# Attention and two MLPs on one core: the second MLP's low pieces on VectorE, casts left to GpSimd, decode slots and splits moved, a 32-byte pad

## The chip, the cores and the metric

The kernel runs on one core of a Trainium2 chip. The metric is the time of one execution in device microseconds. Five engines work side by side: PE (matrix multiply, with its weight loads shown as PEld), DVE (VectorE), ACT (ScalarE), POOL (GpSimd) and SP, which here only issues DMAs. Each engine takes its instructions in the order in which the program put them into its queue.

## The reference

Three stages follow each other: a random-feature attention, an MLP with a leaky rectifier, and a second MLP that multiplies two projections with each other.

```
q_p, k_p = (phi(q_s), phi(k_s))                      # batch 4, heads 8, 576 tokens, 64 wide
x = num / den                                        # -> 2304 tokens x 512
h = x @ w_in;  g = max(h, 0) + alpha * min(h, 0)     # 512 -> 2048
x = g @ w_out                                        # 2048 -> 512
a = x @ w_a;  b = x @ w_b                            # 512 -> 1536, twice
out = (a * b) @ w_out2                               # 1536 -> 512
```

Inputs and outputs are 32-bit; the weights arrive as 64-bit numbers, `raw` in the kernel.

## The kernel before, in words

**Pieces.** Every matrix operand is held as a high piece (a cast to the matmul's 32-bit format) and a low piece (what the cast left over). Each product of two operands is three matmuls: high with high, high with low, low with high. A weight piece therefore fills one slot of 2 x 512 numbers per partition, high half and low half.

**Decode.** `Decoder` turns the 64-bit weights into such slots while the matmuls run. Per weight tile POOL scales one half (`z`, line 196), DVE shifts, masks and multiplies (lines 212, 217, 219, 221), and DVE adds the two parts. For the second MLP the pieces go in groups of two (`quad`) that DVE also combines into sums and differences; then `stage` (line 235) makes the high and the low piece: a POOL cast (line 243), and two slots later a POOL subtract (`pool_tt`, printed with its helper's line 159). There are 20 such stagings in each of three phases of weights, 60 in all. The result goes straight into an open slot, or through the buffer `t` to DRAM and back (`store`, `fetch`). The decoder is a generator: each call of `D_.more(1)`, `D_.go` or `D_.fill` runs it to its next `yield`, which is one decode slot; where those calls stand in the code sets where the decode's instructions stand in each queue.

**First MLP.** Class `Mlp`; each step takes one block f of 128 hidden columns and a chunk of tokens. `first` (line 440) does the 12 matmuls of `h`, ACT and DVE form the rectifier, ACT makes `gh` (line 468), DVE makes `gl` (line 465), and `a_back` (line 498) does the 12 matmuls of each of two steps earlier. The first instance `A` (256 tokens) runs beside the attention until 256 us. The second, `X`, runs from 256 to 553 us in chunks of 512 tokens, but for one of 256 near the middle of its second half. At the last step of a chunk, the matmuls of a step follow only one step behind. `X` runs two decode calls around each rectifier (`D_.fill`) and three between its matmuls.

**Second MLP.** From 553 us on there are nine passes, n = 0 to 8: three weight phases (`ps`), each over three groups of 768 tokens (`tp`). A pass has two `dual`s (j = 0 and 1) and one `back`. A `dual` computes both projections of 256 hidden columns for 768 tokens as 2 x 2 blocks with seven products instead of eight (A11, S1, S2, S4, S3, A12, A22, p = 0 to 6): 7 x 2 x 6 = 84 matmuls of 384 columns (line 1067). What comes out in banks W, E and B is copied by ACT (`s1`, `e5`, `u2`, `u3`, `w7`) and added and multiplied by DVE. The four products `u2`, `s1`, `e5`, `w7` are then split into `gh` (ACT) and `gl` (DVE) by `split`; two of these splits are put into the list `later` and taken out by `drain`, at A11 and S1 of the next dual or at the first tile of `back`. `back` takes six tiles of 128 tokens, 12 matmuls of 512 columns each (line 1138), in which the first three tiles need `gl` of `u2` and `s1` and the last three that of `e5` and `w7`. It adds the earlier phases' part (`opl`, from DRAM) and stores.

**Combine.** Where the next pass takes other tokens (after n = 0, 1, 3, 4, 6, 7), the generator `combine` forms the seven left-hand operands of the next pass: sums on DVE, high pieces on ACT, low pieces for the two row halves k = 0 on DVE and k = 1 on POOL. One step runs after each product of the dual j = 1 from p = 3 on, the others one per tile of `back`.

**Where tiles lie.** Pools without a side fill the memory from the bottom, pools with `side=RIGHT` from the top. In the built program, every tile of the left side starts at a multiple of 64 bytes (slots 0 to 16, 4096 bytes each, the decoder's buffers, the operands of A11, S1 and S2). On the right side, all of `X`'s tiles, slots 17 to 26, `gh` and `gl` of the second MLP and the operands of S4, S3, A12 and A22 start 32 bytes past a multiple of 64; the attention's tiles there are mixed, most of them at multiples of 64. `X` takes its 32 slots in turn: blocks 0 to 7 from slots 0 to 15, blocks 8 to 15 from slots 16 to 24 and then 0 to 6.

Of the kernel before, what the change touches and what calls it, by code (L numbers as in the profile page):

```python
# [18 lines left out]
P = 128  # L19
# [40 lines left out]
def tile_kernel(ctx: ExitStack, tc: tile.TileContext, qT, kT, v1, omT, wbits, alpha, out):  # L60
    nc = tc.nc
    ctx.enter_context(tc.manual_schedule())
    scale = 1.0 / math.sqrt(math.sqrt(D))

    const = ctx.enter_context(tc.tile_pool(name="const", bufs=1))
    w1 = ctx.enter_context(tc.tile_pool(name="w1", bufs=1))
    dec = ctx.enter_context(tc.tile_pool(name="dec", bufs=2))
# [97 lines left out]
    class Decoder:  # L165
# [68 lines left out]
        def stage(self, q, src, cut=None):  # L234

            if cut != 1 and self.open(q):
                self.direct.add(q)
            t = slots[place(q)][2] if q in self.direct else dec.tile([P, 2, 512], F32R, tag="t", name=f"t{q}_{cut}", bufs=3)
            if cut is not None:
                o = 256 * cut if q in self.direct else 0  # L240
                t = t[:, :, o:o + 256]
            self.flush()
            nc.gpsimd.tensor_copy(out=t[:, 0], in_=src)
            load["pool"] += 1.5
            yield
            yield
            pool_tt(t[:, 1], src, t[:, 0].bitcast(F32), ALU.subtract)
            self.due = (q, cut, t)
            yield

# [144 lines left out]
    class Mlp:  # L395
# [48 lines left out]
        def a_front(self, ph, o, n, f, last, mid):  # L444
# [26 lines left out]
            if self.beside:  # L471
                self.beside(high, low)
            else:
                D_.fill()
                high()
                low()
                D_.fill()

        def a_back(self, ph, o, n, f, last_chunk):
            halves = self.pair and o < 2 * CI  # L480
# [463 lines left out]
    def combine(ps, tp):  # L944
# [8 lines left out]
        for i in range(len(A_NAMES) + 2):  # L953
            if i >= 2:
                nm = A_NAMES[i - 2]
                for k in range(2):
                    l = t_(xpools[nm not in EARLY], f"xl{nm}{k}", f"xl{ps}{tp}{nm}{k}", dt=F32R)
                    (pool_tt if k else vec)(l, src[k][nm], high[nm, k].bitcast(F32), ALU.subtract)
                    xs[nm, k] = (high[nm, k], l)
            if 1 <= i <= len(A_NAMES):  # L960
                nm = A_NAMES[i - 1]
# [77 lines left out]
    def split(ps, tp, j, i, c, g):  # L1039

        gh = t_(gp, f"gh{j}{i}{c}", f"gh{ps}{tp}{j}{i}{c}", dt=F32R)
        gl = t_(gp, f"gl{j}{i}{c}", f"gl{ps}{tp}{j}{i}{c}", dt=F32R)
        act(gh, g)
        vec(gl, g, gh.bitcast(F32), ALU.subtract)
        gs[j, i, c] = (gh, gl)

    def dual(ps, tp, j, last, gen=None, g0=0):
        nm_ = f"{ps}{tp}{j}"
# [6 lines left out]
        for p, nm in enumerate(A_NAMES):  # L1055
# [32 lines left out]
            elif nm == "S3":  # L1088
                for m in range(2):
                    act(keep(m, "u3", 1), W[m])  # L1090
                split(ps, tp, j, 0, 1, sb[0]["u2"])
            elif nm == "A12":
                for m in range(2):
                    vec(sb[m]["s1"], banks[m]["B"][:, :TN], sb[m]["s1"], ALU.add)
                vec(sb[0]["s1"], sb[0]["s1"], sb[1]["s1"], ALU.mult)
                for m in range(2):
                    vec(sb[m]["e5"], sb[m]["u3"], sb[m]["e5"], ALU.add)
            else:
                act(keep(0, "w7", 1), W[0])
                split(ps, tp, j, 0, 0, sb[0]["s1"])  # L1100
                vec(sb[0]["w7"], sb[0]["w7"], W[1], ALU.mult)
                vec(sb[0]["e5"], sb[0]["e5"], sb[1]["e5"], ALU.mult)
                later.append(lambda: split(ps, tp, j, 1, 1, sb[0]["e5"]))
                later.append(lambda: split(ps, tp, j, 1, 0, sb[0]["w7"]))
            if nm in ("A11", "S1"):
                drain()
            if gen and p >= g0:
                next(gen, None)
            D_.fetch()
            if last:  # L1110
# [13 lines left out]
    def back(ps, tp, last, gen):  # L1124
        for t in range(2 * TN // P):
# [6 lines left out]
            for j in range(2):  # L1132
                for f in (1, 0):
# [3 lines left out]
                    for w_, r_ in ((gh, wh), (gh, wl), (gl, wh)):  # L1137
                        nc.tensor.matmul(ob, lhsT=w_[:, cs], rhs=r_, start=(n == 0), stop=(n == 11))  # L1138
                        n += 1
                if j == 0 and f == 0:  # L1140
                    D_.more(1)
            passed(12 * 0.227)
            D_.fetch()
            if last and t == 2 * TN // P - 1:
# [17 lines left out]
    for n, (ps, tp) in enumerate(seq):  # L1162
# [3 lines left out]
        for j in range(2):  # L1166
# [7 lines left out]
                    load_o(tp, 0)  # L1174
                    load_o(tp, 1)
            else:
                dual(ps, tp, j, last, gen, 3)
        back(ps, tp, last, gen)
        if gen:
            for _ in gen:  # L1180
# [58 lines left out]
```

## Time and profile before

| what | us |
|---|---|
| median of three runs (992.7 to 994.15) | 992.73 |
| the profiled execution | 989.9 |
| its span, first to last instruction | 988.1 |
| PE busy in the span | 954.2 |
| DVE busy | 698.9 |
| POOL busy | 381.9 |

The profile comes from one execution, 0.3% faster than the median; the span leaves out 1.8 us around the program. Times in the trace count from the span's start. A busy PE is not PE at its peak, since the matmuls overlap and their pace is read from one start to the next.

### The profile page before, as it was taken

The page shows a single profiled execution, that of the slowest core. Times are in us where ns is not written, and L with a number is a line of the kernel's source. Part 1 is how long each engine was busy: PE and PEld are TensorE (multiplying, and loading weights), DVE is VectorE, ACT ScalarE, POOL GpSimd, SP SyncE. Part 2 cuts the span into 40 slices and gives each one's busy share as a digit, 9 for nine tenths or more (in the row PEclk, how much of TensorE's full clock was granted, in tenths as well). Part 3 has the DMA queues.
Part 4 walks back from the last instruction along what each step waited for, and adds up shares of the span by engine and source line. Part 5 has one row for each costly group of instructions (what it writes and reads, how often), then busy time and mean ns, then how long its engine had stood idle before and what let it go on. Part 6 is the DMA issues. An engine that isn't in the chain of part 4 may idle for free.

```text
span 988.1 us, 16903 instructions
## 1 busy us (share of the span) xinstructions
PE 954.2 (97%) x6486; PEld 848.7 (86%) x6486; DVE 698.9 (71%) x1276; ACT 445.0 (45%) x1094; POOL 381.9 (39%) x312
## 2 busy tenths in 40 slices
PE   8899999999999999998999989999999999999998
PEld 7788889999888888888888879899989898979796
DVE  5888855554547768688667988799588995573733
ACT  5877766654444443333333344443343431333340
POOL 3676700000066655437325646264155272030300
PEclk8999999999999999999999999999999999999999
DMA  8544323000123242424546657159827378613112
GB/s 292 175 148 162 113 74 98 24 1 23 43 78 99 80 150 64 135 79 143 198 136 245 233 216 259 62 191 381 292 106 266 118 265 324 242 54 139 63 66 96
DMA packets 54177, 146.55 MB, mean 148 GB/s; under 512 B 5072, under 2 KB 11472, under 8 KB 54096
## 3 DMA queue, kind: packets, MB, share of 16 engines
q1 hardware_dynamic: 53952, 145.34, 42.3%
q8 instruction: 51, 0.84, 0.3%
q14 instruction: 30, 0.25, 0.1%
q10 hardware_dynamic: 144, 0.13, 0.0%
HBM read 98.79 MB, written 46.66 MB: 147 GB/s over the span
## 4 chain that ended last, share of the span: by engine, by line
PE 78%; DVE 13%; ACT 5%; issue 2%; DMA 2%; POOL 0%; SPq 0%; ACTq 0%; DVEq 0%; POOLq 0%
PE y L498 19%; PE h L440 18%; PE o L1138 12%; PE W L1067 12%; PE E L1067 7%; ACT ph L684 3%; PE B L1067 2%; DVE sumS L163 2%; DVE s L163 2%; PE tp L712 1%; DVE e L163 1%; PE kv L697 1%; PE nd L731 1%; DVE gl L163 1%; DMA out<-opl 1%
## 5 line engine op out<-in xcount | busy, mean ns | idle before, releaser
L498 PE MATMUL y<-gh,w 128*128 128x256 f32 (+1 forms) x768 | 205.0, 342 | 3.7 <-ACT gh L468 3.6
L440 PE MATMUL h<-xh,w 128*128 128x256 f32 (+1 forms) x768 | 206.1, 342 | 1.0 <-ACT xh L425 1.0
L196 POOL TENSOR_SCALAR z<-raw 128x512 f32<-128x512 f32 x68 | 111.3, 1639 | 136.7 <-DMA raw<-in_w 75.4
L498 PEld LDWEIGHTS y<-gh,w 128*128 128x128 f32 x768 | 135.4, 191 | 21.1 <-ACT gh L468 4.5
L440 PEld LDWEIGHTS h<-xh,w 128*128 128x128 f32 x768 | 135.1, 189 | 18.1 <-ACT xh L425 1.2
L1138 PE MATMUL o<-w,gh 128*128 128x512 f32 x432 | 137.0, 399 | 0.0
L498 PE MATMUL y<-gl,w 128*128 128x512 f32 (+1 forms) x384 | 130.7, 340 | 0.9 <-DVE gl L465 0.8
L231 POOL TENSOR_TENSOR a<-a,w 128x512 f32<-128x512 f32 x32 | 48.4, 1512 | 213.5 <-ACT w L230 210.7
L440 PE MATMUL h<-xl,w 128*128 128x512 f32 (+1 forms) x384 | 130.1, 339 | 0.5 <-DVE xl L429 0.5
L457 DVE SCALAR_TENSOR_TENSOR h<-u,nalpha,h 128x256 f32<-128x256 f32 (+1 forms) x96 | 59.5, 620 | 83.3 <-ACT h L456 82.2
L1138 PEld LDWEIGHTS o<-w,gh 128*128 128x128 f32 x432 | 81.4, 190 | 19.5 <-ACT gh L155 1.5
L1138 PE MATMUL o<-w,gl 128*128 128x512 f32 x216 | 86.6, 401 | 11.3 <-DVE gl L163 11.3
L455 ACT ACTIVATE u<-h 128x256 f32<-128x256 f32 (+1 forms) x96 | 47.1, 491 | 103.1 <-PE h L440 102.9
L468 ACT ACTIVATE gh<-h 128x256 fp32r<-128x256 f32 (+1 forms) x96 | 47.1, 491 | 99.4 <-DVE h L457 99.4
L498 PEld LDWEIGHTS y<-gl,w 128*128 128x128 f32 x384 | 73.2, 191 | 9.9 <-DVE gl L465 1.6
L440 PEld LDWEIGHTS h<-xl,w 128*128 128x128 f32 x384 | 72.8, 190 | 9.4 <-DVE xl L429 1.0
L465 DVE TENSOR_TENSOR gl<-h,gh 128x256 fp32r<-128x256 f32 (+1 forms) x96 | 53.2, 554 | 24.6 <-ACT gh L468 24.4
L155 ACT ACTIVATE u<-W 128x384 f32<-128x384 f32 x72 | 35.0, 492 | 68.4 <-PE W L1067 67.7
L1138 PEld LDWEIGHTS o<-w,gl 128*128 128x128 f32 x216 | 41.0, 190 | 23.5 <-DVE gl L163 13.9
L217 DVE SCALAR_TENSOR_TENSOR a<-raw,z 128x512 uint32<-128x512 uint32 x68 | 55.6, 818 | 1.9
L221 DVE SCALAR_TENSOR_TENSOR c<-raw,c 128x512 f32<-128x512 uint32 x68 | 49.6, 730 | 2.3
L163 DVE TENSOR_TENSOR opl<-o,opl 128x512 f32<-128x512 f32 x36 | 24.7, 686 | 34.1 <-DMA opl<-opart 25.2
(512 smaller groups left out, 2071.8 us busy)
## 6 DMA issues: line engine op xcount, KB each, us to landing
raw<-in_w SPq DMA_DIRECT2D x68, 512.0 KB, 4.6
w<-store SPq DMA_DIRECT2D x44, 512.0 KB, 7.0
store<-t_None SPq DMA_DIRECT2D x39, 512.0 KB, 2.9
st<-ypart SPq DMA_DIRECT2D x14, 768.0 KB, 6.9
opl<-opart SPq DMA_DIRECT2D x36, 256.0 KB, 3.0
v<-in_v SPq DMA_DIRECT2D x8, 650.0 KB, 5.8
q<-in_qT SPq DMA_DIRECT2D x8, 576.0 KB, 3.7
opart<-op SPq DMA_DIRECT2D x18, 256.0 KB, 2.8
```

Source lines behind the costliest of these rows:

```text
L163: nc.vector.tensor_tensor(out=out, in0=in0, in1=in1, op=op)
L196: nc.gpsimd.tensor_scalar(out=z.bitcast(F32), in0=self.raw[i][:, :, 1].bitcast(F32), scalar1=2.0 ** -112, scalar2=None, op0=ALU.mult)
L217: stt(out=a, in0=H, scalar=0x80000000, in1=z, op0=ALU.bitwise_and, op1=ALU.bitwise_or)
L221: stt(out=c, in0=L, scalar=2.0 ** -52, in1=c, op0=ALU.mult, op1=ALU.mult)
L231: eng.tensor_tensor(out=a, in0=a, in1=hi.bitcast(F32), op=ALU.subtract)
L440: nc.tensor.matmul(hp, lhsT=w_[:, ks], rhs=r_, start=(i == 0), stop=(i == 3 * KT - 1))
L455: nc.scalar.activation(u_, hp, AF.Relu, scale=-1.0)
L457: nc.vector.scalar_tensor_tensor(out=hp, in0=u_, scalar=nalpha[:, f:f + 1], in1=hp, op0=ALU.mult, op1=ALU.add)
L465: nc.vector.tensor_tensor(out=gl, in0=hp, in1=gh.bitcast(F32), op=ALU.subtract)
L498: nc.tensor.matmul(ys[e], lhsT=w_[:, es], rhs=r_, start=(first and i == 0 and head), stop=(last and i == 2 and tail))
L1067: nc.tensor.matmul(out, lhsT=w_[:, ks], rhs=r_, skip_group_check=True, start=(i == 0 and nm in ("A11", "S1", "A12")), stop=(i == 5))
L1138: nc.tensor.matmul(ob, lhsT=w_[:, cs], rhs=r_, start=(n == 0), stop=(n == 11))
```

## The change

All low pieces of `stage` and of `combine` go to DVE, and the high piece of `stage` stays a POOL cast. `back` runs a decode slot after every third matmul and one more at the end of a tile, five instead of two. `X` drops the second of its two `fill` calls once the first MLP's 32 pieces have been begun. In `dual`, the split of `s1` moves: for j = 1 it stands in A12, before and after the `e5` sums; for j = 0 it goes into `later`, which is drained once more, at S2. `combine` in the dual j = 1 starts at p = 2 and leaves out p = 5. A tile of 32 bytes is allocated first on the right side, so that everything else there starts 32 bytes lower: `X`'s tiles, slots 17 to 26, `gh`, `gl` and the right-hand operands now start at multiples of 64, and most of the attention's tiles there 32 bytes past one.

```diff
+    ctx.enter_context(tc.tile_pool(name="pad", bufs=1, side=RIGHT)).tile([P, 8], F32, name="pad")
...
-            pool_tt(t[:, 1], src, t[:, 0].bitcast(F32), ALU.subtract)
+            vec(t[:, 1], src, t[:, 0].bitcast(F32), ALU.subtract)
...
                 low()
-                D_.fill()
+                if self.pair or D_.next <= PB:
+                    D_.fill()
...
-                    (pool_tt if k else vec)(l, src[k][nm], high[nm, k].bitcast(F32), ALU.subtract)
+                    vec(l, src[k][nm], high[nm, k].bitcast(F32), ALU.subtract)
...
+                if j:
+                    low = split(ps, tp, j, 0, 0, sb[0]["s1"])
+                else:
+                    low = lambda: None
+                    later.append(lambda: split(ps, tp, j, 0, 0, sb[0]["s1"])())
                 for m in range(2):
                     vec(sb[m]["e5"], sb[m]["u3"], sb[m]["e5"], ALU.add)
+                low()
             else:
                 act(keep(0, "w7", 1), W[0])
-                split(ps, tp, j, 0, 0, sb[0]["s1"])
...
-            if nm in ("A11", "S1"):
+            if nm in ("A11", "S1", "S2"):
                 drain()
-            if gen and p >= g0:
+            if gen and p >= g0 and not (j and p == 5):
                 next(gen, None)
...
-                if j == 0 and f == 0:
-                    D_.more(1)
+                D_.more(1)
...
-                dual(ps, tp, j, last, gen, 3)
+                dual(ps, tp, j, last, gen, 2)
```

In DVE's queue, the end of the dual j = 1 of pass n = 6 reads as follows before. The names are those of the products (`s1` is printed s10 and s11 for the two projections, then three numbers for ps, tp and j), `sumS2` and `xl21` belong to `combine`, and `gl20100` is the low piece of `s1`.

```order
L163 TENSOR_TENSOR s10_201_9845<-s10_201_9845,s11_201_9847 128x384
L163 TENSOR_TENSOR e50_201_9867<-u30_201_9918,e50_201_9867 128x384
L163 TENSOR_TENSOR e51_201_9869<-u31_201_9920,e51_201_9869 128x384
L163 TENSOR_TENSOR xl21A110_9953<-st1_0_9694,xh21A110_9926 128x384
L163 TENSOR_TENSOR sumS2210_9961<-sumS1210_9930,st1_0_9694 128x384
L163 TENSOR_TENSOR sumS2211_9963<-sumS1211_9932,st1_1_9696 128x384
L163 TENSOR_TENSOR gl20100_9980<-s10_201_9845,gh20100_9979 128x384
```

The same place in DVE's queue in the changed kernel:

```order
L164 TENSOR_TENSOR gl20101_9932<-u20_201_9884,gh20101_9931 128x384
L164 TENSOR_TENSOR xl21A110_9935<-st1_0_9695,xh21A110_9907 128x384
L164 TENSOR_TENSOR xl21A111_9937<-st1_1_9697,xh21A111_9909 128x384
L164 TENSOR_TENSOR sumS2210_9943<-sumS1210_9911,st1_0_9695 128x384
L164 TENSOR_TENSOR sumS2211_9945<-sumS1211_9913,st1_1_9697 128x384
L164 TENSOR_TENSOR s10_201_9842<-B0_201_9947,s10_201_9842 128x384
L164 TENSOR_TENSOR s11_201_9844<-B1_201_9954,s11_201_9844 128x384
L164 TENSOR_TENSOR s10_201_9842<-s10_201_9842,s11_201_9844 128x384
L164 TENSOR_TENSOR e50_201_9864<-u30_201_9927,e50_201_9864 128x384
L164 TENSOR_TENSOR e51_201_9866<-u31_201_9929,e51_201_9866 128x384
L164 TENSOR_TENSOR gl20100_9965<-s10_201_9842,gh20100_9964 128x384
```

The `combine` step that stood between the `e5` sums and `gl20100` now stands ahead of the `s1` sums, one subtract longer.

The second place is the `back` of pass n = 3, second to fourth tile, DVE's queue before (`opl` is the addition at the end of a tile, `xl11` is of `combine`):

```order
L163 TENSOR_TENSOR opl1664_8407<-o1_1664_8618,opl1664_8407 128x512
L163 TENSOR_TENSOR xl11S40_8636<-sumS4110_8576,xh11S40_8612 128x384
L163 TENSOR_TENSOR opl1792_8604<-o1_1792_8647,opl1792_8604 128x512
L163 TENSOR_TENSOR xl11S30_8664<-st1_0_8237,xh11S30_8640 128x384
L163 TENSOR_TENSOR opl1920_8632<-o1_1920_8673,opl1920_8632 128x512
```

The same tiles in DVE's queue in the changed kernel, where `t71` and `t72` are the staging buffers of two weight pieces:

```order
L164 TENSOR_TENSOR opl1664_8373<-o1_1664_8606,opl1664_8373 128x512
L164 TENSOR_TENSOR xl11S40_8625<-sumS4110_8558,xh11S40_8594 128x384
L164 TENSOR_TENSOR xl11S41_8627<-sumS4111_8560,xh11S41_8596 128x384
L164 TENSOR_TENSOR t71_None_8613<-a58_8384,t71_None_8613 128x512
L164 TENSOR_TENSOR opl1792_8586<-o1_1792_8634,opl1792_8586 128x512
L164 TENSOR_TENSOR xl11S30_8654<-st1_0_8222,xh11S30_8629 128x384
L164 TENSOR_TENSOR xl11S31_8656<-st1_1_8224,xh11S31_8631 128x384
L164 TENSOR_TENSOR t72_None_8641<-c58_8385,t72_None_8641 128x512
L164 TENSOR_TENSOR opl1920_8621<-o1_1920_8663,opl1920_8621 128x512
```

Two instructions per tile have come over from POOL, and the low piece of `t71` and `t72` now stands in front of a tile's addition.

POOL's queue for the same four pieces in the changed kernel holds only scalings and casts:

```order
L197 TENSOR_SCALAR z60_8602<-raw60_8382 128x512
L197 TENSOR_SCALAR z61_8604<-raw61_8454 128x512
L244 CAST t71_None_8613<-a58_8384 128x512
L244 CAST t72_None_8641<-c58_8385 128x512
L244 CAST t73_None_8670<-c59_8457 128x512
L244 CAST t74_1_8699<-a59_8456 128x256
```

The scalings `z60` and `z61` of the next two weight tiles stand ahead of the cast of `t71`, as they did before the change.

## Rows read from the trace of the kernel before

**Rows 1.** Page, part 1: busy us, share of the span, instructions.
```profile
PE 954.2 (97%) x6486; PEld 848.7 (86%) x6486; DVE 698.9 (71%) x1276; ACT 445.0 (45%) x1094; POOL 381.9 (39%) x312
```
**Rows 2.** The chain in order of time, in X: start us, us, what.
```profile
389.22 2.80 PE h L440 x12
...
400.25 2.72 PE y L498 x12
```
**Rows 3.** The same view, two backs without a wait (n = 2, n = 5).
```profile
682.53 16.71 PE o L1138 x72
...
825.10 16.79 PE o L1138 x72
```
**Rows 4.** Timeline of PE in the back of n = 2: start us, us, what.
```profile
688.63 0.63 PE L1138 MATMUL o<-w,gh 128*128 128x512 f32 x2
...
689.33 0.62 PE L1138 MATMUL o<-w,gh 128*128 128x512 f32 x2
...
690.02 0.63 PE L1138 MATMUL o<-w,gh 128*128 128x512 f32 x2
```
**Rows 5.** Windows over the six backs beside a combine: length, busy us; first, fifth, sum.
```profile
583.86:605.45 21.59, 18.29 (x73) 14.46 (x73) 20.08 (x23) 8.81 (x18) 18.14 (x16) 0.92 0.35 132
...
871.03:889.71 18.68, 17.16 (x74) 13.38 (x74) 15.26 (x27) 6.57 (x14) 6.72 (x6) 1.00 0.22 71
...
sum 115.41, PE 104.07 PEld 81.37 DVE 106.01 ACT 44.35 POOL 62.56; mean PE 17.35 PEld 13.56 DVE 17.67 ACT 7.39 POOL 10.43
```
**Rows 6.** PE's waits from 550 us on: total us, times, longest.
```profile
PE o L1138 <- DVE gl L163: 11.3, 6, 3.3
PE E L1067 <- ACT e L155: 0.6, 1, 0.6
```
**Rows 7.** Timeline around the start of the back of n = 6 (871.03): DVE, POOL.
```profile
865.65 0.56 DVE L163 TENSOR_TENSOR u<-u,u 128x384 f32<-128x384 f32 x1
...
868.06 0.56 DVE L163 TENSOR_TENSOR gl<-u,gh 128x384 fp32r<-128x384 f32 x1 [1.85 <-ACT gh L155]
...
868.54 1.84 DVE L163 TENSOR_TENSOR sumS<-st 128x384 f32<-128x384 f32 x2
...
868.93 1.03 POOL L159 TENSOR_TENSOR xl21A<-st,xh21A 128x384 fp32r<-128x384 f32 x1 [19.63 <-PE B L1067]
...
870.30 1.01 DVE L163 TENSOR_TENSOR s<-B,s 128x384 f32<-128x384 f32 x2
...
871.08 1.02 POOL L159 TENSOR_TENSOR xl21S<-sumS,xh21S 128x384 fp32r<-128x384 f32 x1 [1.11 <-ACT xh21S L155]
...
871.35 1.16 DVE L163 TENSOR_TENSOR s<-s,s 128x384 f32<-128x384 f32 x1
...
872.43 1.01 DVE L163 TENSOR_TENSOR e<-u,e 128x384 f32<-128x384 f32 x2
...
873.84 1.01 DVE L163 TENSOR_TENSOR sumS<-sumS,st 128x384 f32<-128x384 f32 x2
...
874.77 0.55 DVE L163 TENSOR_TENSOR gl<-s,gh 128x384 fp32r<-128x384 f32 x1
```
**Rows 8.** Timeline of PE in X, at the end of its 256-token chunk.
```profile
459.35 0.38 PE L498 MATMUL y<-gh,w 128*128 128x256 f32 x1 [3.25 <-ACT gh L468]
```
**Rows 9.** Windows, as rows 5; PEclk, DMA share, GB/s end the line.
```profile
455.00:462.00 7.00, 3.55 (x20) 3.15 (x19) 6.76 (x13) 2.49 (x6) 2.39 (x3) 0.83 0.65 218
```
**Rows 10.** Groups from 256 us on, POOL: count, busy us, mean ns, idle before.
```profile
L196 POOL TENSOR_SCALAR z<-raw 128x512 f32<-128x512 f32 x49 | 81.6, 1667 | 122.2 <-DMA raw<-in_w 61.0 <-DVE e L163 19.4 <-DVE c L163 16.6
L159 POOL TENSOR_TENSOR t_None<-a,t_None 128x512 fp32r<-128x512 f32 x20 | 27.6, 1379 | 1.5
...
L243 POOL CAST t_None<-c 128x512 fp32r<-128x512 f32 x19 | 16.5, 870 | 6.8 <-DVE c L163 6.8
```
**Rows 11.** Timeline of DVE at 752 us, a decode addition of 512 columns.
```profile
752.58 0.69 DVE L163 TENSOR_TENSOR a<-a,c 128x512 f32<-128x512 f32 x1
```
**Rows 12.** The chain's end, in order of time.
```profile
970.85 3.34 DMA out<-opl
...
974.58 3.27 DMA out<-opl
```

More of the change, by code (lines that the diff above doesn't have):

```diff
@@ L1043, in split @@
         act(gh, g)
-        vec(gl, g, gh.bitcast(F32), ALU.subtract)
         gs[j, i, c] = (gh, gl)
+        return lambda: vec(gl, g, gh.bitcast(F32), ALU.subtract)
     def dual(ps, tp, j, last, gen=None, g0=0):
@@ L1090, in dual @@
                     act(keep(m, "u3", 1), W[m])
-                split(ps, tp, j, 0, 1, sb[0]["u2"])
+                split(ps, tp, j, 0, 1, sb[0]["u2"])()
             elif nm == "A12":
@@ L1095, in dual @@
                 vec(sb[0]["s1"], sb[0]["s1"], sb[1]["s1"], ALU.mult)
+                if j:
[3 more added lines that the diff above has]
+                    later.append(lambda: split(ps, tp, j, 0, 0, sb[0]["s1"])())
                 for m in range(2):
                     vec(sb[m]["e5"], sb[m]["u3"], sb[m]["e5"], ALU.add)
+                low()
             else:
                 act(keep(0, "w7", 1), W[0])
-                split(ps, tp, j, 0, 0, sb[0]["s1"])
                 vec(sb[0]["w7"], sb[0]["w7"], W[1], ALU.mult)
                 vec(sb[0]["e5"], sb[0]["e5"], sb[1]["e5"], ALU.mult)
-                later.append(lambda: split(ps, tp, j, 1, 1, sb[0]["e5"]))
-                later.append(lambda: split(ps, tp, j, 1, 0, sb[0]["w7"]))
-            if nm in ("A11", "S1"):
+                later.append(lambda: split(ps, tp, j, 1, 1, sb[0]["e5"])())
+                later.append(lambda: split(ps, tp, j, 1, 0, sb[0]["w7"])())
+            if nm in ("A11", "S1", "S2"):
                 drain()
-            if gen and p >= g0:
+            if gen and p >= g0 and not (j and p == 5):
                 next(gen, None)
```

## The prediction

> **What bounds the kernel now.** The shares of the page come first: PE is busy for 954.2 of 988.1 us [rows 1]. So only two things can move the time much: PE's pace, and the stretches in which it waits. DVE and POOL matter only through these.
>
> The pace is read from the chain in order of time. In X, 12 matmuls of 512 columns take 2.80 us in one stretch and 2.72 us in the next [rows 2], with nothing waiting in either. The stretches alternate with the slots that hold the weights: 2.80 where they lie in slots 0 to 16 (left side), 2.72 where they lie in slots 17 to 24 (right side); the tokens' operands lie right in both. The same shows inside one `back`: six matmuls from 688.63 to 690.02, of which the first three take 0.70 us and the last three 0.69 [rows 4], and only the last three read a right-hand slot. The `back` of n = 2, where a quarter of the matmuls read a right-hand slot, takes 16.71 us, that of n = 5 with none 16.79 [rows 3]. So a matmul of 512 columns takes 233 ns where weights and moving operand lie on different sides and 227 ns where both lie right.
>
> The waits come next. From 550 us on, PE waits for `gl` six times, 11.3 us in all [rows 6]. The windows over the six `back`s give the full loss: they sum to 115.41 us [rows 5], against 6 x 16.75 without a wait [rows 3], so 14.9 us. That is more than the listed waits, since the pipeline has to fill again and, at n = 0, the granted clock fell to a mean of 0.92 in that window [rows 5]. The timeline of n = 6 shows why: `gl` of `s1` ends at 875.32, while PE got there at 871.03 + 11 x 0.23 = 873.56. DVE is late there for two reasons. A `combine` step stands between the `e5` sums and this `gl`, and DVE operations with both inputs in SBUF stretch while POOL subtracts: `sumS` takes 0.92 instead of 0.5 and `s1` x `s1` 1.16 instead of 0.56, while the sums that read a PSUM bank keep 0.5 [rows 7]. X has one such wait, 3.25 us at 459.35 [rows 8], behind which the clock stayed at half for a while (a mean of 0.83 over 7 us [rows 9]): with that and the refill, about 5.5 us.
>
> **The pad.** Before, left means a multiple of 64 bytes and right means 32 past one; after it, all these tiles are at multiples of 64. I take the residue, not the side, as what sets the pace: in each fast stretch both operands share it. X has 64 groups of 12 whose weights lie left (two chunks with 16, four with 8), each 0.08 us too long: 5.1 us. In the 256-token chunk the order is the reverse, 117 against 120 ns, by the same reading of 92 matmuls; that costs 0.3. The `back`s of n = 0 to 2 have 54 slow matmuls each, n = 3 to 7 have 72: 522 x 6.6 ns = 3.5 us. The last `back` counts nothing, because its end hangs on a chain of DMAs: the stores go out 3.73 us apart [rows 12], longer than a tile of 2.8 us. For 384 columns I see no difference. Sum: 8.3 us gained, bounds 0 (side decides) and 9. What the pad does to the attention's small matmuls I take as nothing, between a gain of 1 and a loss of 2: their pace before is the same for `v` at either residue, and the engines wait for each other there anyway.
>
> The Trainium skill (SBUF — State Buffer, "SBUF: two separate sides") says that on the engines' side only the port pair shared by DVE and GpSimd causes contention and that PE never waits on anyone. By that, an address could not change PE's pace and this term would be 0 instead of 8.3. The trace has the two paces all the same [rows 2, 4], so I keep the term; that rule is the rival "pad idle" below.
>
> **The move of `s1`'s split and of the `combine` step.** For j = 1 the `gl` of `s1` no longer stands behind the step that was at p = 5. From rows 7, the new queue at n = 6: after `gl` of `u2` at 868.54, two subtracts and two sums at 0.47 apiece (two take 1.01 with the last one's end), 1.9; two bank sums 1.05, the product 0.6, two `e5` sums 0.94, `gl` 0.55. It ends at 873.6 instead of 875.32, and PE gets there at 873.5 with the faster pace. The first step's sums fall into the 1.85 us in which DVE idles ahead of 868.06. What is left of the wait is 0.1, with the refill 0.2, at n = 6 and 7. At n = 0, 1, 3 and 4 the decode stands in the same queue: one or two operations of 0.4 to 0.7 between `u2` and this `gl`, and the third drain at S2 makes DVE wait for ACT once more. I take 1.0, 0.5, 1.3 and 0.8 there. Left in all: 4.0 of 14.9, so 10.9 gained; bounds 4 (only n = 6, 7 and part of the rest) and 13.5. For j = 0 the split goes from A22 to the next A11, off a place where DVE is full; the one wait on `e` goes with it [rows 6], 0.9 with its refill.
>
> **POOL's subtracts to DVE.** 60 pieces of `stage` and 49 of `combine` cost DVE 0.69 [rows 11] and 0.47 [rows 7] apiece, so 41 + 23 = 64 us more; and each POOL subtract of 1.0 to 1.4 us [rows 7, 10], beside which DVE stretched, is gone. Over one `back` of n = 6, DVE was busy for 15.26 us [rows 5] though its 13 instructions take 6.9 us at the unstretched durations; with five subtracts more it needs 9.3. So on balance DVE does not get fuller; it is filled at other places. What hides this is slack: a `dual` is 14.6 us, a `back` 16.3. At n = 3, j = 1, its instructions add up to 17.4 us, and in the `back`s of n = 3 and 4 to 15.4 and 17.7, because of the five slots. So DVE runs some 5 to 7 us behind at the ends of these passes and catches up in the next dual, where nothing of it is needed at once, but that `w7` must release its bank 3.1 us after the next dual begins.
>
> **The wait that is added.** The low piece on DVE has to wait for POOL's cast, and the two scalings of the next weight tiles stand ahead of that cast. A scaling takes 1.67 us and the cast 0.87; POOL waited 61.0 us for `raw` since 256 us [rows 10]. DVE meets the low piece three slots after the scalings, 1.6 us of PE in a `back`, 2 to 4 in a dual, against 2 x 1.67 + 0.87 = 4.2. So it can block for 1 to 2.5 us a quad, and behind it in DVE's queue stand a tile's addition and the bank sums. Cover: DVE being behind already, and PE needing nothing of it soon. I charge 2 us of PE for this and for the fuller places together; bounds 0 and 10.
>
> **The fewer slots in X.** Four decode slots a step instead of five, with the same number of DVE microseconds in a quad and no POOL subtracts beside them. In the 256-token chunk, two steps of 2.9 us still meet some 9 us of DVE work, so that `gl` comes about 1.8 us late instead of 3.3; at n = 6 a wait of that length left the clock at a mean of 1.00 [rows 5]. I take 2.2 us left of 5.5: 3.3 gained, bounds 0 and 5.5. The pieces that X no longer decodes are made up in the `back`s: the order shows the last piece of a phase before the pass that needs it, so no forced decode.
>
> **Sum.** 8.3 + 10.9 + 0.9 + 3.3 - 2 = 21.4 us off the profiled 989.9, so 968.5. The profiled run is 2.8 below the median; on the median's footing 992.7 - 21.4 = 971.3, say 971.
>
> **Rivals.**
> *Pad idle:* the side (or the tiles' distance) sets the pace, not the residue. For it: the two coincide before, so the trace can't part them. Against it: nothing but the residue seems likely to bind a slot 16 to one pace and a slot 17 to another. 971 + 8.3 = 980.
> *DVE too full:* the five slots a tile put DVE so far behind that the waits at n = 0, 1, 3 and 4 stay, and the banks are released late. For it: 17.4 and 17.7 us of work in 14.6 and 16.3. Against it: before, DVE was busy for 17.67 of a mean 19.2 us there [rows 5] and no dual suffered. 10.9 becomes 3.5 and the 2 becomes 4: 980.
> *DVE hangs on POOL, slower than before:* the scalings' waits for `raw`, 61.0 us [rows 10], now block DVE through the casts, in X and in n = 0 to 5. They decide once over 21 of the 61 us reach PE; half of them gives 971 + 30 = 1001. Against it: PE takes only `gl` and banks from DVE, with several us to spare.
>
> **How the numbers follow.** Forecast 971: 0.62, with its own range of 963 to 977. Pad idle 0.15 and DVE too full 0.14, both at 980, within 974 to 985. Slower 0.04. Better than 963, with every wait gone, 0.05. The range from 963 to 983 leaves out about 2 in 10. A measurement of this kernel can tell about 0.2%, 2 us, from no change: faster by more 0.94, within it 0.02, slower 0.04.
>
> **What would show it.** In the changed profile, groups of 12 in X should take 2.72 us throughout, and an unwaited `back` 16.3 to 16.4; 2.80 and 16.8 there mean pad idle. PE's waits for `gl` at the start of the `back`s should be near 0 at n = 6 and 7 and under 1.5 elsewhere; waits of 2 us or more at n = 3 and 4 mean DVE too full. DVE waiting for POOL casts, followed by PE waits in the duals, means the third rival. The forecast is wrong on the good side if X's wait is gone, and on the bad side if new waits of PE on DVE appear inside X or the duals.

## The result

| | median us | lowest to highest | runs |
|---|---|---|---|
| before | 992.99 | 992.7 to 994.15 | 4 |
| changed | 978.0 | 976.68 to 981.6 | 4 |

The ratio is 0.9854, with a 95% interval from 0.9829 to 0.9878: 15.0 us less. The forecast was 971, 21.7 us less, with a range from 963 to 983. Sign and range held, and 6.7 us of the expected gain are missing. The profiled execution took 981.6 us, the slowest of the four; its span is 979.8.

One thing in the description ahead of the prediction was read wrongly. The decode call in `back` stands in the loop over j, behind the loop over f. So a tile has three slots, one behind each six matmuls and one at its end, and not five. The sums of DVE's work that the prediction gives with the five slots (15.4, 17.4 and 17.7 us) are no rows of a trace, and no run here shows them.

### The profile page after: what moved, and what is told of

Same layout as the page of the kernel before. It is cut to its first block, busy times and chain, and to the rows that moved or that the text cites. A ratio compares the mean times of both kernels' runs of the same rounds, so it can differ in the third digit from the quotient of the medians.

```text
span 979.8 us, 16903 instructions
## 1 busy us (share of the span) xinstructions
PE 947.9 (97%) x6486; PEld 849.8 (87%) x6486; DVE 704.7 (72%) x1384; ACT 442.2 (45%) x1094; POOL 249.6 (25%) x204
## 4 chain that ended last, share of the span: by engine, by line
PE 67%; DVE 18%; ACT 6%; DMA 5%; issue 4%; POOL 1%; SPq 0%; DVEq 0%; POOLq 0%; ACTq 0%
PE h L441 18%; PE y L500 18%; PE W L1069 9%; PE o L1145 8%; PE E L1069 5%; ACT ph L686 3%; DMA raw<-in_w 2%; PE B L1069 2%; DVE e L164 1%; DVE a L218 1%; DVE s L164 1%; PE tp L714 1%; DVE sumS L164 1%; PE kv L699 1%; DVE gl L164 1%
## 5 line engine op out<-in xcount | busy, mean ns | idle before, releaser
L500 PE MATMUL y<-gh,w 128*128 128x256 f32 (+1 forms) x768 | 202.3, 338 | 1.0 <-ACT gh L469 0.9
L441 PEld LDWEIGHTS h<-xh,w 128*128 128x128 f32 x768 | 135.0, 189 | 16.4 <-ACT xh L426 1.2
L1145 PE MATMUL o<-w,gh 128*128 128x512 f32 x432 | 134.8, 393 | 4.8 <-ACT gh L156 4.8
L1145 PEld LDWEIGHTS o<-w,gh 128*128 128x128 f32 x432 | 81.5, 190 | 22.4 <-ACT gh L156 6.1
L156 ACT ACTIVATE s<-W 128x384 f32<-128x384 f32 x36 | 17.7, 492 | 78.5 <-PE W L1069 67.8
L218 DVE SCALAR_TENSOR_TENSOR a<-raw,z 128x512 uint32<-128x512 uint32 x68 | 51.5, 758 | 1.9
```

The lines of the kernel that those rows point to most:

```text
L156: nc.scalar.activation(out, in_, AF.Copy)
L218: stt(out=a, in0=H, scalar=0x80000000, in1=z, op0=ALU.bitwise_and, op1=ALU.bitwise_or)
L441: nc.tensor.matmul(hp, lhsT=w_[:, ks], rhs=r_, start=(i == 0), stop=(i == 3 * KT - 1))
L500: nc.tensor.matmul(ys[e], lhsT=w_[:, es], rhs=r_, start=(first and i == 0 and head), stop=(last and i == 2 and tail))
```

## The profile after

Part 1 of the page of the changed kernel, to be read beside [rows 1]:

```profile
PE 947.9 (97%) x6486; PEld 849.8 (87%) x6486; DVE 704.7 (72%) x1384; ACT 442.2 (45%) x1094; POOL 249.6 (25%) x204
```

PE is busy 6.3 us less for the same 6486 matmuls. DVE has 108 more instructions and is busy only 5.8 us more, and POOL has lost 132 us.

The pace, in the chain in order of time, at the place of [rows 2] (start us, us, what):

```profile
380.29 2.72 PE h L441 x12
383.01 5.44 PE y L500 x24
388.45 2.72 PE h L441 x12
391.17 2.72 PE y L500 x12
```

Every group of 12 takes 2.72 us; the 2.80 of [rows 2] is gone. The six `back`s beside a `combine`, in the columns of [rows 5] (stretch, length, busy us of the five engines, PEclk, DMA share, GB/s), in the order n = 0, 1, 3, 4, 6, 7:

```profile
581.98:600.10 18.12, 16.95 (x74) 13.37 (x73) 17.75 (x36) 8.91 (x19) 3.92 (x4) 1.00 0.35 133
629.24:646.11 16.87, 16.75 (x73) 13.36 (x73) 16.60 (x34) 8.91 (x19) 1.97 (x3) 1.00 0.26 79
720.76:743.14 22.38, 18.56 (x74) 14.50 (x73) 22.28 (x43) 6.31 (x14) 5.79 (x6) 0.92 0.27 98
774.20:791.02 16.82, 16.70 (x73) 13.36 (x73) 16.58 (x32) 6.32 (x14) 2.44 (x2) 1.00 0.26 82
867.51:883.92 16.41, 16.41 (x74) 13.44 (x73) 14.00 (x29) 6.31 (x14) 0.00 (x0) 1.00 0.27 81
913.06:929.47 16.41, 16.41 (x73) 13.44 (x73) 14.21 (x29) 6.32 (x14) 0.00 (x0) 1.00 0.26 81
sum 107.01, PE 101.78 PEld 81.46 DVE 101.42 ACT 43.07 POOL 14.12; mean PE 16.96 PEld 13.58 DVE 16.90 ACT 7.18 POOL 2.35
```

Without a wait a `back` takes 16.36 us now (n = 2 and 5, from the first matmul of it to that of the next pass). Those of n = 6 and 7 are at that, where the waits that the move of `s1`'s split was aimed at are gone; n = 1 and 4 are within 0.5 of it, and n = 0 takes 1.8 more. That of n = 3 takes 22.38 against 19.12 before. It is one of four places where time comes back. PE's waits from 546 us on (total us, times, longest):

```profile
PE o L1145 <- ACT gh L156: 4.8, 2, 3.7
PE W L1069 <- DVE yp L531: 3.3, 1, 3.3
PE E L1069 <- ACT e L156: 1.8, 2, 1.5
PE W L1069 <- ACT s L156: 1.0, 1, 1.0
```

[rows 6] had 11.3 us on `gl` and 0.6 on `e`. Where these four stand is told by the windows (columns as above) of the first dual of n = 0 and of the second duals of n = 4 and 5, none of which waited for anything worth 1 us before:

```profile
546.50:567.42 20.92, 17.65 (x85) 17.32 (x84) 17.60 (x34) 7.20 (x16) 4.03 (x5) 0.84 0.52 188
757.72:774.20 16.48, 15.11 (x86) 14.47 (x86) 13.49 (x26) 7.13 (x16) 4.46 (x5) 1.00 0.53 188
805.61:822.00 16.39, 14.90 (x85) 14.51 (x85) 15.90 (x30) 6.16 (x14) 4.07 (x3) 1.00 0.93 338
```

A dual without a wait takes 14.6. So they cost 6.3, 1.9 and 1.8 us, and n = 3 costs 6.0 beyond 16.4; at n = 0 and n = 3 the granted clock fell as well (0.84 and 0.92). Together that is 16 us, for which the prediction had charged 2, with 1.3 more kept for n = 3.

Where the wait of n = 3 comes from is read in the queues ahead of it. POOL (timeline; the bracket holds the idle time before and what ended it):

```profile
688.97 1.51 POOL L197 TENSOR_SCALAR z<-raw 128x512 f32<-128x512 f32 x1 [12.12 <-DMA raw<-in_w]
690.43 0.61 POOL L244 CAST t_None<-a 128x512 fp32r<-128x512 f32 x1
699.09 1.59 POOL L197 TENSOR_SCALAR z<-raw 128x512 f32<-128x512 f32 x1 [8.05 <-DMA raw<-in_w]
701.01 1.52 POOL L197 TENSOR_SCALAR z<-raw 128x512 f32<-128x512 f32 x1 [0.33 <-DMA raw<-in_w]
702.47 0.62 POOL L244 CAST w<-a 128x512 fp32r<-128x512 f32 x1
```

DVE at the same time:

```profile
691.07 0.69 DVE L164 TENSOR_TENSOR t_None<-a,t_None 128x512 fp32r<-128x512 f32 x1 [8.56 <-POOL t_None L244]
...
703.12 1.06 DVE L164 TENSOR_TENSOR w<-a,w 128x512 fp32r<-128x512 f32 x1 [3.82 <-POOL w L244]
...
725.54 0.56 DVE L164 TENSOR_TENSOR s<-s,s 128x384 f32<-128x384 f32 x1
...
726.96 0.55 DVE L164 TENSOR_TENSOR gl<-s,gh 128x384 fp32r<-128x384 f32 x1
```

And ACT and PE at the start of the `back` of n = 3:

```profile
726.14 0.52 ACT L156 ACTIVATE gh<-s 128x384 fp32r<-128x384 f32 x1 [5.71 <-DVE s L164]
```

```profile
726.71 0.74 PE L1145 MATMUL o<-w,gh 128*128 128x512 f32 x2 [3.70 <-ACT gh L156]
```

POOL waits for a raw weight tile, the cast stands behind that scaling, and DVE's low piece stands behind the cast. DVE is idle for 8.56 and 3.82 us while its work piles up. Between the second of these waits and the product `s` at 725.54 it pauses only once for longer than 0.1 us (0.59 us, for `gh`), so 22 us later the delay is still there: ACT waits 5.71 us for `s` and PE 3.70 us for the `gh` made from it; `gl` follows at 726.96. Before the change DVE had no wait on POOL from 256 us on; now its waits there are 18.3 us on casts of `t_None`, 3.8 on `w` and 1.2 on `t`. In the second dual of n = 4 one of them, 4.77 us, ends at 760.02, before PE's waits there. Ahead of PE's wait in that of n = 5 the longest is 0.64 us, and ahead of the first dual of n = 0 there is none. So those two are another matter, which the experiments take up.

## The experiments

All times are medians; each ratio is to the kernel before on the same chip, where that took 991.8 to 992.9 us.

**The pad alone and all but the pad.**

```diff
+    ctx.enter_context(tc.tile_pool(name="pad", bufs=1, side=RIGHT)).tile([P, 8], F32, name="pad")
```

> The kernel before with the 32-byte pad alone. Theory (address residue sets PE's pace): every group of 12 matmuls of 512 columns in X takes 2.72 us, an unwaited back 16.3 to 16.4 us, X is 4.8 us shorter (the 256-token chunk 0.3 longer counted), the backs 3.5; in all 8.3 us less, about 984.5, with the waits for gl at the start of the backs left as they are (11 us listed). Rival (the gain in X came from the absent POOL subtracts and the dropped decode slots, the pad does nothing): 992.7, groups of 2.80 and 2.72 side by side as before.

> The changed kernel without the pad. Theory (residue): groups of 2.80 us return in X where the weights lie in slots 0 to 16, backs 16.7 to 16.8, about 8.3 us more than the changed kernel's 978.0, so 986. Rival (pad does nothing): 978. The waits of PE in the second MLP should be those of the changed kernel in either case (n = 0 first dual 3.3 to 3.6, back of n = 3 about 4, second duals of n = 4 and 5 about 1.8 each), unless they depend on PE's own pace.

Measured: 983.63 (ratio 0.990, 0.988 to 0.992), 9.2 less than before; and 985.0 (0.9919, 0.9904 to 0.9934), 7.0 more than the changed kernel. The chain in order of time of the kernel with the pad alone, and of the changed kernel without it:

```profile
388.73 2.72 PE h L441 x12
391.45 2.72 PE y L499 x12
394.17 5.44 PE h L441 x24
```

```profile
389.81 2.80 PE h L440 x12
392.61 2.79 PE y L499 x12
395.40 5.44 PE h L440 x24
```

The pad alone makes the pace even, and without it the 2.80 is back, with no other edit in play. The side of each tile is the same in all four kernels, so it is the start address that counts, and the rival "pad idle" is out; shifts other than 32 bytes were not tried. What was not expected is a small gain in the first duals: from n = 3 on they take 14.59 with the pad and 14.66 to 14.74 without it.

**The moves alone.** The kernel before with the splits and `combine` moved as in the change; no pad, and POOL keeps its subtracts.

```diff
-                split(ps, tp, j, 0, 0, sb[0]["s1"])
...
+                    low = split(ps, tp, j, 0, 0, sb[0]["s1"])
...
-            if gen and p >= g0:
+            if gen and p >= g0 and not (j and p == 5):
```

> The kernel before with the moves inside the second MLP alone: the split of s1 in A12 (j = 1) or at the next A11 (j = 0), the third drain at S2, combine from p = 2 on and not at p = 5. No pad, all POOL subtracts kept. Theory (the order of DVE's queue makes gl late): the waits for gl at the starts of the six backs fall from 11.3 us listed to 4 or less, the backs' sum by 8 to 10 us, and the wait on e (0.6) goes: 983 to 985. Rival (DVE is late because its operations stretch beside POOL's subtracts, whatever the order): the waits stay above 7 us and the time is 989 to 992.

Measured: 982.32 (0.9901, 0.9866 to 0.9935), 9.8 less than the 992.08 of before. The windows over the same six `back`s, the one of n = 7 and the sum:

```profile
914.31:931.44 17.13, 17.04 (x73) 13.39 (x73) 13.61 (x25) 6.39 (x14) 6.07 (x5) 1.00 0.24 77
sum 106.22, PE 102.75 PEld 80.27 DVE 95.92 ACT 42.36 POOL 56.98; mean PE 17.13 PEld 13.38 DVE 15.99 ACT 7.06 POOL 9.50
```

From 115.41 [rows 5] to 106.22: 9.2 us out of the `back`s, with POOL still busy for 57 us in them. So the order of DVE's queue made `gl` late; to take the subtracts off POOL was not needed for these 9.2 us.

**Both together.**

> The kernel before with the pad of e1 and the moves of e5 together, nothing else of the change. Theory (the two gains add, 9.2 and 9.8, and the rest of the change, low pieces on DVE, X's dropped call, the extra slots, costs more than it brings): 973 to 974, which is 4 to 5 us less than the whole changed kernel's 978. Rival (the two overlap, since a faster PE reaches the starts of the backs earlier and waits there longer): 976 to 978.

Measured: 973.96 (0.9821, 0.9785 to 0.9858), 18.6 less. The two add up, and these two parts alone gain 4 us more than the whole change, though the intervals of the two kernels overlap. So something may be lost in the rest of the change.

**What X's dropped call is worth.**

```diff
-                if self.pair or D_.next <= PB:
-                    D_.fill()
+                D_.fill()
```

> The changed kernel with the second decode call of X's steps kept to the end. Theory (the dropped call took away DVE work in the 256-token chunk, worth 3.3 us): the wait near 450 us, 0.6 us now, is 2 to 3.3 again with the clock at half behind it, X 3 to 4 us longer; at n = 0 the decode is further ahead, so that the first dual's wait for the y sums (3.3 us, 6.3 with the clock) may shrink; 978 to 982. Rival (it is the POOL subtracts, gone from beside DVE, that cured the 256-token chunk): wait under 1 us as now, and time 978 or, with n = 0 mended, 973.

Measured: 988.74 (0.9964, 0.9947 to 0.998), 10.7 more than the changed kernel and well above what was expected. In X it is as the theory had it, and more. PE's waits in X's narrow chunk, in this kernel (first two rows) and then in the changed one:

```profile
456.31 0.38 PE L499 MATMUL y<-gh,w 128*128 128x256 f32 x1 [3.12 <-ACT gh L469]
457.33 0.58 PE L499 MATMUL y<-gl,w 128*128 128x256 f32 x1 [0.64 <-DVE gl L466]
```

```profile
453.98 0.38 PE L500 MATMUL y<-gh,w 128*128 128x256 f32 x1 [0.56 <-ACT gh L469]
```

From X's first matmul to that of the second MLP it is 294.5 us with the call and 286.7 without, 7.8 apart. The POOL subtracts are gone in both, so it is the call. Part of it is the clock: from 445 to 465 us the granted clock was 0.83 with the call, against 0.91 in the kernel before and 1.00 in the changed one. The rest of the 10.7 fell in the second MLP: its first dual is short there (15.0 us), but the `back` of n = 0 takes 27.0 and the second dual of n = 2 21.5, and DVE waits 23.3 us for POOL's casts of `t_None`. Decode that runs ahead does not thin these waits; it moves them.

**Two slots a tile.**

```diff
-                D_.more(1)
+                if j == 0 and f == 0:
+                    D_.more(1)
```

> The changed kernel with two decode slots per tile of back, as before the change, where it has three (one behind each six matmuls and one at the end). Theory (the extra slots crowd DVE): the wait of 4.1 at the start of the back of n = 3 falls under 2, those of n = 4 and 5 fall too, 4 to 6 us less: 972 to 974. Rival (with X's second call dropped the pieces are then decoded too late, and the rest is forced into the queue where a phase begins): a new PE wait of over 3 us at the start of n = 3 or n = 6, 980 or more. Second rival (the casts behind the scalings are all that matters): within 2 us of 978.

Measured: 989.41 (0.9977, 0.9959 to 0.9995), 11.4 more than the changed kernel. The waits in the second duals of n = 4 and 5 are gone, as the theory had it, but the `back` of n = 3 grew from 22.4 to 24.0 us. The first rival holds, one place further on than it had it: in the `back` of n = 6, PE stands for 9.77 us for a weight piece that POOL has only just cast.

```profile
876.69 1.52 PE L1145 MATMUL o<-w,gh 128*128 128x512 f32 x2 [9.77 <-POOL w L244]
```

POOL's cast of it began at 876.03, after 12.21 us of waiting for DVE's part of the decode. With two slots and X's call kept, the kernel with pad and moves alone has no such wait (16.8 us at n = 6). That fits that the third slot pays for what X no longer decodes; since that kernel differs in POOL's subtracts too, it is not shown by itself.

**Casts ahead of the scalings.** In `quad`, and likewise in `single`:

```diff
-            self.start(i + 2)
-            if self.kind(i + 2) == "quad":
-                self.start(i + 3)
             yield
...
-            yield from self.stage(q3, a1[:, g], m)
+            end = self.stage(q3, a1[:, g], m)
+            next(end)
+            self.start(i + 2)
+            if self.kind(i + 2) == "quad":
+                self.start(i + 3)
+            yield
+            yield from end
```

> The changed kernel, but POOL's scalings for the next one or two weight tiles are put behind the casts of the tile in hand instead of ahead of them. Theory (DVE hangs on POOL: its low pieces wait for casts that stand behind scalings that wait for raw): DVE's waits for POOL's casts from 256 us on, 23 us in all in the changed kernel's profile, fall under 5; the wait of 4.1 at the start of the back of n = 3 falls under 1, those of 1.9 and 1.8 in the second duals of n = 4 and 5 under 0.5; with the clock that fell behind the first, 8 to 9 us less: 969 to 971. Rival (DVE too full): the waits for casts go, but the wait at n = 3 stays at 3 to 4, and the time within 2 us of 978. Second rival: DVE now waits as long for the scaling itself at its shift, and nothing is won, 978. The wait of n = 0 (3.3, DVE late at X's end with decode) stays in all three.

Measured: 969.04 (0.9757, 0.9743 to 0.9772), 9.0 less than the changed kernel. The window over the `back` of n = 3, and POOL's group of scalings ahead of it (timeline):

```profile
715.65:732.90 17.25, 16.94 (x74) 13.36 (x73) 17.15 (x35) 6.31 (x14) 1.38 (x2) 1.00 0.27 84
```

```profile
677.64 1.52 POOL L197 TENSOR_SCALAR z<-raw 128x512 f32<-128x512 f32 x1
683.76 1.52 POOL L197 TENSOR_SCALAR z<-raw 128x512 f32<-128x512 f32 x1 [4.60 <-DMA raw<-in_w]
```

22.38 became 17.25, and the six `back`s together take 99.98 instead of 107.01. POOL waits once for `raw` from 256 us on (4.6 us), against 94.3 us in 16 waits in the changed kernel. DVE has the same instructions as there. "DVE too full" is out as the cause at n = 3, and "DVE hangs on POOL" is shown there and at n = 4, whose second dual takes 14.6 us now. In the second dual of n = 5 it is not: that was to lose its wait too and takes 16.84 us, 16.39 in the changed kernel, with DVE busy for 16.30 of them. With two slots a tile it was 14.6, which points to DVE being too full there. DVE still waits for a scaling now and then, 4.7 us in all; that is the second rival's wait, but a short one. The wait of n = 0 stayed (2.6 us), as was expected of all three. It stays with the low pieces on POOL as well (3.1, next experiment), and it is absent where X keeps its call: there the first dual takes 14.6 to 15.0 us, in the kernel with the call put back and in those with the moves alone. So it comes with the dropped call, not with the casts.

**The low pieces back on POOL.**

```diff
-            vec(t[:, 1], src, t[:, 0].bitcast(F32), ALU.subtract)
+            pool_tt(t[:, 1], src, t[:, 0].bitcast(F32), ALU.subtract)
```

> The changed kernel with the 60 low pieces of stage back on POOL, all else as changed. Theory (DVE hangs on POOL): no DVE wait for POOL left, the waits at n = 3, 4 and 5 under 1, 0.5, 0.5: 8 us less by these; DVE operations with both inputs in SBUF stretch again beside 20 or so POOL subtracts after 256 us (0.55 to about 1.0 us), which gives back 1 to 3 us at the starts of the backs of n = 0, 1, 3, 4: 971 to 973. Rival (moving the low pieces to DVE is what opened the backs): the waits at the backs' starts of n = 0, 1, 3, 4 return to 2 us or more each: 978 or more.

Measured: 978.65 (0.9855, 0.9824 to 0.9885), the same as the changed kernel. No DVE wait for a cast is left, and yet nothing is won: the `back`s of n = 0 and n = 3 take 20.8 and 21.1 us and the second dual of n = 5 takes 18.1. The rival came true in its time and at n = 0 and 3, but not at n = 1 and 4 (16.9 and 16.4). If the removed waits were worth the 9.0 us that the casts first gained, DVE's stretch beside POOL's subtracts, expected at 1 to 3 us, took back as much; no run parts the two.

**No decode at X's end.** The kernel with the casts first, and in `a_back`:

```diff
-                if not self.pair and e < 3 and not last:
+                if not self.pair and e < 3 and not last and not (last_chunk and f >= FA - 3):
```

> The kernel of e3_cast_first, without the six decode calls in the last two groups of X's second matmuls. Theory (DVE reaches the y sums late because six decode slots stand ahead of them): the wait for the y sums at the start of n = 0, 2.6 us there, falls under 0.3, and the first dual of n = 0 takes 14.6 to 15 us in place of 19.1: 964 to 965. Rival (the decode is only displaced and is late again further on, at the back of n = 0 or at n = 3): 968 to 970, with the lost time at the new place.

Measured: 966.26 (0.974, 0.971 to 0.9771), 2.8 less than with the casts first alone and 26 less than before; it is the fastest kernel of this study, though the intervals of these two ratios overlap. Windows over the first dual of n = 0 and the second of n = 4:

```profile
544.01:559.69 15.68, 15.14 (x86) 14.49 (x84) 15.48 (x31) 7.19 (x16) 4.71 (x5) 1.00 0.48 174
742.65:760.67 18.02, 15.16 (x86) 14.52 (x85) 17.50 (x34) 7.98 (x18) 6.26 (x6) 1.00 0.64 246
```

Both are right in part: the first dual of n = 0 falls from 19.1 to 15.7, and the shifted decode brings 3.4 us at n = 4.

**Three tries for more.**

> The kernel of e8_cast_first_xlast, with X's second decode call kept in the chunks of 512 tokens and dropped only in the one of 256. Theory (X's narrow chunk is where the call hurts, the wide ones have DVE time to spare; decode that is ahead thins the second MLP): X as long as in e8 (the wait near 450 us stays at 0.6), the waits of the second dual of n = 4 (3.4 us with the pipeline's refill, 1.6 in the back behind it) and of n = 1's back (0.7) fall to under 2 together: 961 to 963. Rival (as in e7, the displaced decode makes DVE wait for POOL at other places): 966 or more, with DVE's waits for POOL over 10 us.

> The kernel of e10_wide_fill with two decode slots per tile of back in place of three. By the changed order DVE's own durations add up to at most 15.7 us in any dual and 14.5 in any back. Theory (what is left of the waits is DVE too full): 960 to 962, no PE wait over 1 us after 553. Rival (the decode runs late and a phase begins with a wait, as in the two-slot kernel e6): 966 or more, at n = 3 or n = 6.

Measured: 976.44 (0.9846, 0.9805 to 0.9886) and 973.63 (0.9817, 0.9784 to 0.985). X is as short as hoped (286.3 and 286.2 us), and in the second of them no pass but n = 0 loses more than 1.3 us. But in both the `back` of n = 0 takes 26 us, and in the first the second dual of n = 4 takes 19.4. POOL and DVE ahead of the `back` of n = 0, in the kernel with two slots:

```profile
572.77 0.40 POOL L244 CAST t<-a 128x256 fp32r<-128x256 f32 x1 [18.82 <-DMA store<-t_None]
```

```profile
573.20 0.86 DVE L164 TENSOR_TENSOR t<-a,t 128x256 fp32r<-128x256 f32 x1 [8.92 <-POOL t L244]
```

This time the cast waits for a free buffer `t`, whose store to DRAM was issued behind two loads of `st`, three fetches of weight pieces and a load of `raw`. Casts first does not help against that. The first rival holds (DVE waits 15.2 us for casts of `t`); the second holds in its time, but not in its place, which was n = 3 or 6.

> The kernel of e9_before_pad_split (the kernel before, pad, moves of the splits and of combine) with three more edits: combine's low pieces all on DVE, X's second decode call dropped in the 256-token chunk alone, and no decode calls in the last two groups of X. The low pieces of stage stay on POOL, so that DVE has no cast to wait for; two slots per tile. Theory (what the change loses, it loses by DVE waiting for POOL's casts, and the rest of it is sound): no DVE wait for a cast; against e9 the wait near 455 us with the slow clock behind it goes (4 to 5 us), the one at X's end too (3 to 4), and the backs of n = 3 and 4, 19.0 and 18.0 there, come under 17.5: 962 to 966. Rival (POOL's subtracts stretch DVE as much as they relieve it, as in e4_low_on_pool): waits of 2 us or more at the backs of n = 0, 3 or 4, 968 or more, and the kernel of e8_cast_first_xlast with 966.3 stays the best.

Measured: 979.6 (0.9887, 0.9869 to 0.9905). The rival holds: no wait for a cast, but the `back`s of n = 0, 1 and 4 take 22.6, 22.3 and 21.7 us. DVE ahead of n = 0, with POOL's subtracts beside it:

```profile
571.93 2.52 DVE L164 TENSOR_TENSOR xl01A<-st,xh01A 128x384 fp32r<-128x384 f32 x2
574.38 2.53 DVE L164 TENSOR_TENSOR sumS<-sumS,st 128x384 f32<-128x384 f32 x2
576.83 1.01 DVE L164 TENSOR_TENSOR s<-B,s 128x384 f32<-128x384 f32 x2
577.87 1.26 DVE L164 TENSOR_TENSOR s<-s,s 128x384 f32<-128x384 f32 x1
```

```profile
572.57 1.48 POOL L160 TENSOR_TENSOR t_None<-a,t_None 128x512 fp32r<-128x512 f32 x1
573.99 0.94 POOL L244 CAST t_None<-c 128x512 fp32r<-128x512 f32 x1
575.01 1.48 POOL L160 TENSOR_TENSOR t_None<-c,t_None 128x512 fp32r<-128x512 f32 x1
...
577.46 1.26 POOL L160 TENSOR_TENSOR t_None<-c,t_None 128x512 fp32r<-128x512 f32 x1
```

Pairs that take 1.02 us alone take 2.5. The pair behind them, which reads a PSUM bank, keeps 1.01, though the next subtract begins within it; the product `s`, with both inputs in SBUF, then takes 1.26 beside that subtract, against 0.56 alone. Ahead of n = 1 and 4 it is the same: four subtracts each, and beside them pairs of up to 1.77 and 2.53 us.

## Why the prediction was right, and where it was not

**The pad, 8.3 us (0 to 9).** Measured 9.2 on the kernel before and 7.0 on the changed one. The place and the mechanism are shown by the two paces with the pad alone and without it. In the profiles X is 4.9 us shorter by the pad in the changed kernel and 4.7 with the moves, against 4.8 in the prediction; in the kernel before it is 2.5, with a new PE wait of 1.5 us near X's end. The small excess of 9.2 over 8.3 is within the intervals; part of it may be the 0.1 us in each of the later first duals, which the prediction put at nothing.

**The moves, 10.9 + 0.9 us (4 to 13.5).** Measured 9.8 alone. Right in mechanism, a little high in size. The queue of n = 6 came out as worked out, without a wait; n = 3 and 4 kept 2.6 and 1.5 to 1.6 us where POOL's subtracts stayed.

**X, 3.3 us (0 to 5.5).** Too low: from the first matmul of X to that of the second MLP, 296.2 us became 286.7, where pad and call together were to give 8.1. With the pad in both, the call is 7.8 us. The prediction said that X has one such wait; the kernel with the call has a second, short one near 548 us (0.6 us), and the clock behind the first stayed down longer than before (0.83 against 0.91 from 445 to 465 us, by estimate 1.6 us of those 20). These two make up most of the 2.3 us over the upper bound of 5.5. But the term also put the price of the dropped call elsewhere at nothing, and the first dual of n = 0, 14.6 before, takes 20.9.

**POOL's subtracts to DVE.** "On balance DVE does not get fuller" holds nearly: 704.7 us busy against 698.9.

**The added wait, 2 us (0 to 10).** This is the step that failed. It took a scaling at 1.67 us and said that DVE could block for 1 to 2.5 us a quad. The waits were up to 8.6 us. Of the 16 us at the four places, 7.9 hang on the casts (n = 3 and 4) and 1.8 are at a place where DVE is full (n = 5): 9.7, for which 2 was charged, still inside the bounds of 0 to 10. The other 6.3, at n = 0, belong to X's dropped call and were charged nowhere. The prediction had the row that says so, POOL's 61.0 us of waiting for `raw` [rows 10], and left it to the rival with a chance of 0.04, since DVE had slack. Against this, casts first gives back 9.0 and no decode at X's end another 2.8. With the casts first the whole stands at 969.0, 23.8 below before, near the 23.4 that the forecast's terms make without that charge. That nearness is in part luck: X's call brought 4.5 us more than its term, which offsets most of what n = 0 cost (its first dual takes 19.1 us with the casts first).

**The rivals.** "Pad idle" is out. "DVE too full" foretold the sign, a wait of 2 us or more at n = 3, but not the cause: with DVE's work unchanged and the casts ahead, the wait went. "DVE hangs on POOL" had the cause and a price that was too high by far to make the kernel slower than before. The sign named for "DVE too full", a PE wait of 2 us or more at n = 3, came by the other's cause, so it does not tell the two apart; what was left at n = 5 fits "DVE too full". What tells them apart is DVE's own idle time on POOL's casts, over 20 us earlier, which the prediction named for the third rival alone.

**The last `back`.** As predicted it counts nothing: it is 0.43 us shorter, and the stretch from its end to the span's end is 0.46 longer (4.66 against 4.19).

**The four runs.** They spread over 4.9 us, against 1.5 before. In the profiled one, the slowest, 2.3 us were lost before 45 us already, in which the granted clock from 10 to 20 us was 0.61 against 0.88 before. What makes that stretch differ from run to run was not tried.

**What stays open.** In the fastest kernel 3.4 us at the second dual of n = 4 and 1.6 in the `back` behind it remain. DVE is full there (17.5 us of work in 18.0), and every shift of the decode that was tried moved such a heap to another place. What the low pieces on DVE are worth by themselves, once the casts stand first, was not run alone.

## What to carry to other kernels

Before an operation is moved to an engine on which others hang, look at what its new producer waits for, as far back as the DMA: the price of the new wait is set by the producer's own waits (here a scaling that waited 12.1 us for a transfer), not by its duration (a cast of 0.6 us). Slack on average does not pay for it, since here work that piled up behind a wait was still late 22 us later. An in-order queue should hold what others wait for ahead of what itself waits for a transfer; here that order alone was worth 9 us. And two of the change's parts, an address and a place in a queue, brought at least as much as the whole (18.6 against 15.0 us, with overlapping intervals), which is why a change is best timed in its parts.

## What the runs showed of the hardware

PE's pace depends on where weights and moving operand start: groups of 12 matmuls of 512 columns take 2.80 us when one starts at a multiple of 64 bytes and the other 32 past it, and 2.72 when both agree, in the kernel before and in the changed one alike, though DVE and POOL do different work beside it. For 384 columns the same shift moves a first dual by 0.1 us. The Trainium skill (SBUF — State Buffer, "Who interferes with whom") says that PE never waits on anyone; the prediction took from this rule a rival by which the pad is worth nothing, and the pad was worth 7 to 9 us.

POOL and DVE: from 256 us on in the kernel of the last try, DVE's additions, subtracts and products of 384 columns with both inputs in SBUF took 0.55 us beside an idle POOL and 1.1 on average beside a POOL subtract (51 instructions), 1.65 at the most; those that read a PSUM bank took 0.55 in either case. The Trainium skill (SBUF — State Buffer, "Who interferes with whom") says that a DVE instruction with two SBUF inputs contends with a GpSimd instruction that reads SBUF; the trace agrees, with 0.55 alone and up to 1.65 beside it. So one POOL subtract of 1.48 us can cost DVE more than the 0.69 us which the subtract takes on DVE itself.
